# One fixed sequence for the MLP steps of all batches, with the attention of the next batch at set distances between them

## The chip, the cores and the metric

The kernel runs on one core of a Trainium2 chip. The metric is the device time of one execution in microseconds, taken from the first to the last instruction with what the launch adds around it. Before the change the median of three runs is 771.01 us (767.04 to 771.77). The profile is of one execution that took 770.31 us, with a span of 768.5 us from its first to its last instruction.

## The reference, cut to what matters

Four batches, 768 positions, 8 heads of 48, model width 384. Three layers follow one another, each batch by itself:

```python
f = sigmoid(f_logit)                                   # gated linear attention
for t in range(768):
    state = f[t, :, None] * state + outer(k[t], v[t])
    y[t] = q[t] @ state
x = y                                                  # (768, 384)
u = x + V.T @ (U.T @ x)                                # low-rank mix over positions
x = u + relu(u @ w_ch1) @ w_ch2                        # MLP, 384 -> 1536 -> 384
h = gelu(x @ w_in); a, g = halves(h)                   # second MLP with a spatial gate
out = x + (a * (w_sg @ layernorm(g) + b_sg)) @ w_out
```

The products of the two MLPs are made in three passes: each operand is held as a rounded high part and the rest (names ending in h and l), and high by high, high by low and low by high are added. So one logical matmul of the MLP is three in the trace. The weights arrive as 64-bit numbers and are narrowed on the chip: ScalarE scales the high word, VectorE shifts the low word and merges the two, then ScalarE rounds the high part and GpSimd subtracts for the rest.

## The kernel before, in words

The positions of a batch are cut into six chunks of 128 for the attention and into two halves of 384 for the MLP. The activations lie transposed in `xT[b]` (width on the partitions).

Attention of one chunk is five functions. `a_scan` (L308) takes the sigmoid on ScalarE, a backward and a forward scan of products on VectorE with three short VectorE instructions between them (`gmin` L328, `fall` L330, the reciprocal L331), and scales k and q by the results, mostly on GpSimd (L337, L338). `a_scores` (L343) multiplies k by q into two PSUM banks, masks them on VectorE (`am`, L353) and transposes k. `a_out` (L364) makes the outputs of the chunk from the state and from the masked scores, and the chunk's own k by v; ScalarE and GpSimd split the result into high and low part (`xh`, `xl`). `a_state` (L398) updates the state T on VectorE. `a_xt` (L412) turns the output into `xT`. `low_rank_sum` adds up the low-rank product after chunks 2 and 5 (every chunk for batch 0), and `low_rank_out` adds it to `xT`. `make_hl` then splits a half of `xT` into high and low part (`uh`, `ul`): three ScalarE and three GpSimd instructions.

The MLP of one half is 12 steps. Step f multiplies block f of the first weights with `uh` and `ul` into a bank `h` (9 matmuls, L79), applies ReLU on ScalarE (`ah`, L513), takes the rest on VectorE (`al`, L514), and then issues the second product (9 matmuls into three banks `ch`, L505) of the step before, from that step's `ah` and `al`. The second product of the last step of a half is issued after the loop, followed by three additions into `xT` (L530). After each step `fill(f)` issues other work. There are eight PSUM banks: two `h`, three `ch`, three `at`; the attention of batches 1 to 3 uses the three `at` banks.

What sets the order: every engine works its own queue in order. Inside a block of manual schedule the instructions of an engine keep the order in which the program issues them. Outside such a block a planner puts them in order from its own estimates when the program is built. It may also put instructions of later code between those of a block. Two blocks are manual before the change: batch 0's attention with the loading of weights (L538 to L585), and the MLP of batch 0's first half (L606 with `order`). Everything after is the planner's: the rest of the MLP with the attention of batches 1 to 3 (`attention_steps`, dealt out by counts in L598 to L602), the narrowing of the last weights during batch 3 (`fill` L626, `spatial` L632), and the second MLP (L713 on). `fill` of batch 0's first half also narrows the first weights ahead: `bank_middle`, `use_last` and `bank_first` for blocks f+3, f+2 and f+4.

Batch 0's sigmoid goes into a PSUM bank, that of batches 1 to 3 in place into the loaded tile, so the two can be told apart in the trace. A chunk of `fqk` and `v` is loaded two chunks ahead, into one of three buffers each.

Of the kernel before, what the change touches and what calls it, by code (L numbers as in the profile page):

```python
# [34 lines left out]
LIMIT = 1e-15  # L35
UNIT = 384
# [14 lines left out]
def kernel(  # L51
# [79 lines left out]
    def fast(st):  # L131
# [176 lines left out]
        def a_scan(b, c):  # L308
# [22 lines left out]
            ready = vec.reciprocal(fone[:, :, 0:1], gmin[:, i, :, None])  # L331
# [4 lines left out]
            with tc.issue_after(ready.ins) if b == 0 else nullcontext():  # L336
                pool.tensor_tensor(k, k, g.rearrange("p h t -> p (h t)"), op=ALU.mult)  # L337
# [126 lines left out]
        def attention_steps(b):  # L464
            def first():
                a_scan(b, 0)
            yield first
            for c in range(NCH):
                def s1(c=c):
                    a_scores(b, c)  # L470

                def s2(c=c):
                    if c + 1 < NCH:
                        a_scan(b, c + 1)
                    a_out(b, c)
                    nb, nc2 = divmod(b * NCH + c + 2, NCH)
                    if nb < B:
                        load(nb, nc2)

                def s3(c=c):  # L480
                    if c + 1 < NCH:
                        a_state(b, c)
                    a_xt(b, c)
                    low_rank_sum(b, c)
                yield s1
                yield s2
                yield s3

            def low(hf):
                low_rank_out(b, hf)  # L490
            yield lambda: low(0)
            yield lambda: low(1)

        def mlp(b, hf, fill, order=nullcontext):
            if (b, hf) not in hl:
                make_hl(work, b, hf)
            u = hl.pop((b, hf))
            ch = [bank("ch", [128, HT]) for _ in range(KD)]
            pend = None
# [7 lines left out]
            with order():  # L507
                for f in range(KF1):
                    hp = bank("h", [128, HT])
# [28 lines left out]
        with tc.manual_schedule():  # L538
# [14 lines left out]
            for c in range(NCH):  # L553
# [7 lines left out]
                if c:  # L561
                    a_xt(0, c - 1)
# [362 lines left out]
```

## Time and profile before

| | |
|---|---|
| median of 3 runs | 771.01 us |
| profiled execution, its span | 770.31 us, 768.5 us |
| TensorE matmul busy | 724.8 us (94%) |
| VectorE busy | 447.8 us (58%) |
| ScalarE, GpSimd busy | 258.3 us, 259.0 us (34% each) |
| mean granted TensorE clock | 0.969 |

Matmuls are pipelined, so busy time tells only that something was in the array; a step of 18 matmuls is judged by the time from its start to the next. Four stretches follow one another: batch 0's attention to 65.6 us, the MLP stream with the attention of the next batches and the last weights to 513.0 us, then the second MLP to the end. Within the MLP stream the starts of the halves can be found by the `h` matmuls: 65.6, 122.2, 205.9, 266.6, 321.1, 377.7, 433.9 and 475.4 us.

### The profile page before, as it was taken

The page shows a single profiled execution, that of the slowest core. Times are in us where ns is not written, and L with a number is a line of the kernel's source. Part 1 is how long each engine was busy: PE and PEld are TensorE (multiplying, and loading weights), DVE is VectorE, ACT ScalarE, POOL GpSimd, SP SyncE. Part 2 cuts the span into 40 slices and gives each one's busy share as a digit, 9 for nine tenths or more (in the row PEclk, how much of TensorE's full clock was granted, in tenths as well). Part 3 has the DMA queues.
Part 4 walks back from the last instruction along what each step waited for, and adds up shares of the span by engine and source line. Part 5 has one row for each costly group of instructions (what it writes and reads, how often), then busy time and mean ns, then how long its engine had stood idle before and what let it go on. Part 6 is the DMA issues. An engine that isn't in the chain of part 4 may idle for free.

```text
span 768.5 us, 11556 instructions
## 1 busy us (share of the span) xinstructions
PE 724.8 (94%) x4613; PEld 688.0 (90%) x4613; DVE 447.8 (58%) x789; ACT 258.3 (34%) x520; POOL 259.0 (34%) x273
## 2 busy tenths in 40 slices
PE   7977798998899999999999889999999999999996
PEld 5965688998899999999999789999989999999996
DVE  7857995655645555444533882138667447538632
ACT  2324551231322223222222551225444334524410
POOL 3312572323512122321201840326634435435130
PEclk8979899997999999999999999999999999999999
DMA  9991001131111131011100440210001001000101
GB/s 248 306 380 29 1 1 47 51 90 48 46 49 47 47 89 52 1 48 48 49 1 1 129 140 11 72 42 0 1 1 63 1 1 61 1 1 18 46 1 66
DMA packets 17934, 44.84 MB, mean 58 GB/s; under 512 B 2160, under 2 KB 9968, under 8 KB 17872
## 3 DMA queue, kind: packets, MB, share of 16 engines
q1 hardware_dynamic: 17872, 44.03, 18.9%
q8 instruction: 38, 0.62, 0.4%
q14 instruction: 24, 0.20, 0.1%
HBM read 39.30 MB, written 4.72 MB: 57 GB/s over the span
## 4 chain that ended last, share of the span: by engine, by line
PE 74%; DVE 15%; DMA 6%; ACT 2%; issue 1%; POOL 1%; SPq 1%; DVEq 0%; POOLq 0%; ACTq 0%
PE ps_h L79 22%; PE ps_ch L505 14%; PE ps_ch L79 12%; PE ps_at L79 12%; PE ps_at L373 4%; DMA fqk<-in_fqk_dram 3%; PE ps_at L349 2%; DVE fqk L332 2%; PE ps_at L370 2%; DVE z L248 1%; DVE g L325 1%; DMA xT<-in_fqk_dram 1%; DMA raw<-in_w_dram 1%; DVE al L514 1%; DVE z L101 1%; DVE raw L238 1%
## 5 line engine op out<-in xcount | busy, mean ns | idle before, releaser
L505 PE MATMUL ps_ch<-ah,w 128*128 128x384 f32 x576 | 163.2, 339 | 2.1 <-DVE xT L530 1.1
L79 PE MATMUL ps_h<-uh,w 128*128 128x384 f32 x576 | 126.0, 352 | 3.6 <-ACT w L277 2.6
L505 PE MATMUL ps_ch<-al,w 128*128 128x384 f32 x288 | 98.7, 343 | 15.9 <-DVE al L514 15.8
L514 DVE SCALAR_TENSOR_TENSOR al<-ps_h,ah 128x384 fp32r<-128x384 f32 x96 | 53.1, 554 | 98.6 <-ACT ah L513 97.5
L505 PEld LDWEIGHTS ps_ch<-ah,w 128*128 128x128 f32 x576 | 106.9, 190 | 3.0 <-ACT ah L513 3.0
L79 PEld LDWEIGHTS ps_h<-uh,w 128*128 128x128 f32 x576 | 102.1, 194 | 6.7 <-ACT w L277 3.3
L513 ACT ACTIVATE ah<-ps_h 128x384 fp32r<-128x384 f32 x96 | 46.9, 489 | 135.7 <-PE ps_h L79 130.5
L145 POOL TENSOR_TENSOR xl<-x,xh 128x384 fp32r<-128x384 f32 x18 | 21.0, 1165 | 156.6 <-ACT xh L144 156.6
L505 PEld LDWEIGHTS ps_ch<-al,w 128*128 128x128 f32 x288 | 54.9, 190 | 19.9 <-DVE al L514 19.8
L79 PE MATMUL ps_h<-ul,w 128*128 128x384 f32 x288 | 67.0, 340 | 0.0
L145 POOL TENSOR_TENSOR ul<-xT,uh 128x384 fp32r<-128x384 f32 x45 | 46.3, 1058 | 33.8 <-ACT uh L144 32.9
L145 POOL TENSOR_TENSOR gtl<-t,gth 128x384 fp32r<-128x384 f32 x32 | 32.7, 1024 | 73.6 <-ACT gth L144 73.6
L79 PEld LDWEIGHTS ps_h<-ul,w 128*128 128x128 f32 x288 | 53.0, 193 | 0.0
L337 POOL TENSOR_TENSOR fqk<-fqk,g 112x512 f32<-112x512 f32 x21 | 27.1, 1290 | 57.6 <-DVE gmin L328 26.8
L144 ACT ACTIVATE gth<-t 128x384 fp32r<-128x384 f32 x32 | 16.8, 525 | 78.0 <-DVE t L702 78.0
L353 DVE TENSOR_TENSOR am<-ps_at,mask 128x512 f32<-128x512 f32 x48 | 30.7, 682 | 16.4 <-PE ps_at L349 16.4
L145 POOL TENSOR_TENSOR vnl<-t,vnh 128x512 fp32r<-128x512 f32 x24 | 31.0, 1292 | 17.8 <-ACT vnh L144 17.8
L79 PE MATMUL ps_ch<-w,vnh 128*128 128x384 f32 x144 | 36.6, 335 | 0.1
L279 POOL TENSOR_TENSOR w<-z,w 128x384 fp32r<-128x384 f32 x24 | 24.8, 1054 | 35.0 <-ACT w L277 35.0
L79 PE MATMUL ps_at<-w,vnh 128*128 128x384 f32 x144 | 36.6, 334 | 0.0
L373 PE MATMUL ps_at<-v,am 128*128 128x48 f32 x288 | 35.9, 280 | 0.0
L373 PEld LDWEIGHTS ps_at<-v,am 128*128 128x128 f32 x288 | 35.4, 200 | 0.0
(218 smaller groups left out, 1555.4 us busy)
## 6 DMA issues: line engine op xcount, KB each, us to landing
fqk<-in_fqk_dram SPq DMA_DIRECT2D x19, 679.0 KB, 4.7
raw<-in_w_dram SPq DMA_DIRECT2D x24, 384.0 KB, 8.9
out_dram<-xT SPq DMA_DIRECT2D x24, 192.0 KB, 2.0
v<-in_v_dram SPq DMA_DIRECT2D x21, 192.0 KB, 3.3
raw<-in_w_in_dram SPq DMA_DIRECT2D x8, 384.0 KB, 3.5
z<-in_w_sg_dram SPq DMA_DIRECT2D x12, 192.0 KB, 2.4
xT<-in_fqk_dram SPq DMA_DIRECT2D x3, 679.0 KB, 11.6
raw<-in_w_out_dram SPq DMA_DIRECT2D x4, 384.0 KB, 3.2
```

Source lines behind the costliest of these rows:

```text
L79: pe.matmul(ps, lhsT=l, rhs=r, start=(i == 0), stop=(i == n - 1))
L144: act.activation(hi, src, ACTF.Copy)
L145: eng.tensor_tensor(lo, src, hi.bitcast(F32), op=ALU.subtract)
L279: pool.tensor_tensor(t[:, 1], s, t[:, 0].bitcast(F32), op=ALU.subtract)
L332: vec.tensor_tensor_scan(flat_f, f, fone.rearrange("p h t -> p (h t)"), 1.0, op0=ALU.mult, op1=ALU.max)
L337: pool.tensor_tensor(k, k, g.rearrange("p h t -> p (h t)"), op=ALU.mult)
L349: pe.matmul(sc[j][:, p, :], lhsT=e["k"][rows, p, :], rhs=e["q"][rows, p, :], start=True, stop=True)
L353: vec.tensor_tensor(am, sc[j], mask[:, None, :].to_broadcast([128, NP, C]), op=ALU.mult)
L373: pe.matmul(y[:, h * D:(h + 1) * D], lhsT=e["am"][h % 2][:, h // 2, :], rhs=vv[:, h * D:(h + 1) * D], start=(c == 0 and h == 0), stop=(h = ...
L505: pe.matmul(ch[d], lhsT=l, rhs=r, start=(f == 0 and i == 0), stop=(f == KF1 - 1 and i == 2))
L513: act.activation(ah, hp, ACTF.Relu)
L514: vec.scalar_tensor_tensor(al, hp, 0.0, ah.bitcast(F32), op0=ALU.max, op1=ALU.subtract)
```

## The change

One manual block is opened before the first load and closed only after the last step of batch 3 (`fixed.close()`); the last second product comes after it, then the second MLP as before. The MLP of all batches is 96 steps. The second product of a step is held in `pend` and issued in the next step across halves and batches too, and the additions into `xT` follow each bank's last matmul. For batches 0 to 2 a table says which step (0 to 23) issues which stage of the next batch's attention: chunk c is scanned at step `at[c]`, scored two steps later, put out three later with the load of chunk c+3 (before: c+2), `xT` and the low-rank sum four later; the state follows the output, or the scan of the next chunk if that is later. `at` is 9, 11, 12, 14, 16, 17 for batch 1 and 0, 3, 7, 10, 14, 17 for batches 2 and 3. Within a step the order is by rank: 0 narrowing of weights, 1 scan, 2 output, 3 scores and state, 4 the rest, 5 and 6 low-rank output and split. In batch 3 the raw data of a step are fetched two steps ahead. For batch 0 the scaling of k on GpSimd now waits for the reciprocal of the scan by a semaphore.

```diff
-            with tc.issue_after(ready.ins) if b == 0 else nullcontext():
-                pool.tensor_tensor(k, k, g.rearrange("p h t -> p (h t)"), op=ALU.mult)
+            decayed = pool.tensor_tensor(k, k, g.rearrange("p h t -> p (h t)"), op=ALU.mult)
+            if b == 0:
+                tc.add_manual_dep(decayed.ins, turned.ins.name,
+                                  mybir.DependencyInfo(mybir.DependencyClass.Sync, mybir.DependencyReason.DATA))
...
+        pend = [lambda: None]
+        def mlp(b, hf, fill):
             u = hl.pop((b, hf))
+            ch = []
             def second(f, a):
+                if f == 0:
+                    ch.extend(bank("ch", [128, HT]) for _ in range(KD))
                 for d in range(KD):
...
+                    if f == KF1 - 1:
+                        dst = xT[b][:, d, hf * HT:(hf + 1) * HT]
+                        vec.tensor_tensor(dst, ch[d], dst, op=ALU.add)
+            for f in range(KF1):
+                hp = bank("h", [128, HT])
...
+                act.activation(ah, hp, ACTF.Relu)
+                vec.scalar_tensor_tensor(al, hp, 0.0, ah.bitcast(F32), op0=ALU.max, op1=ALU.subtract)
+                pend.pop()()
+                pend.append(lambda f=f, a=(ah, al): second(f, a))
+                fill(hf * KF1 + f)
...
+        fixed = st.enter_context(ExitStack())
+        fixed.enter_context(tc.manual_schedule())
...
+            if b == 0:
+                for f in range(KF1):
+                    put(f, 0, narrow_ahead, f)
+                put(KF1 - 4, 4, load, 1, 2)
+            put(KF1 // 2, 5, make_hl, work, b, 1)
+            at = BEGIN[b > 0]
             for c in range(NCH):
+                put(at[c], 1, a_scan, b + 1, c)
+                put(at[c] + 2, 3, a_scores, b + 1, c)
+                put(at[c] + 3, 2, out_and_load, b + 1, c)
                 if c + 1 < NCH:
+                    put(max(at[c] + 3, at[c + 1]), 3, a_state, b + 1, c)
+                put(at[c] + 4, 4, rest, b + 1, c)
+            put(2 * KF1 - 2, 5, low_rank_out, b + 1, 0)
+            put(2 * KF1 - 2, 6, make_hl, work, b + 1, 0)
+            put(2 * KF1 - 1, 5, low_rank_out, b + 1, 1)
...
+        def fill_last(i):
+            if i < KF1:
+                hi, lo, _, at = todo[i]
+                c = slice(at, at + UNIT)
+                split(hi[:, c], lo[:, c], narrow_last(narrow_first(stage, here.pop(i), 128, UNIT))[0])
+            else:
+                split(*wsg[i - KF1], here.pop(i))
+            fetch_last(i + 2)
...
+            if i == KF1 // 2:
+                make_hl(work, B - 1, 1)
+            elif i == 2 * KF1 - 1:
+                make_hl(work2, 0, 0)
+                make_hl(work2, 0, 1)
...
+        for hf in range(2):
+            mlp(B - 1, hf, fill_last)
+        fixed.close()
+        pend.pop()()
```

## Rows read from the trace of the kernel before

**Rows 1.** The page's first part: busy time of each engine, share and instructions.

```profile
PE 724.8 (94%) x4613; PEld 688.0 (90%) x4613; DVE 447.8 (58%) x789; ACT 258.3 (34%) x520; POOL 259.0 (34%) x273
```

**Rows 2.** Windows: length, busy time (instructions) by engine, granted clock, DMA share, GB/s.

```profile
0.00:65.60 65.60, 55.15 (x411) 44.67 (x412) 44.43 (x85) 20.46 (x41) 16.82 (x25) 0.87 0.92 282
...
46.00:57.00 11.00, 10.60 (x55) 9.44 (x55) 4.84 (x11) 1.97 (x5) 1.95 (x2) 0.55 1.05 390
...
65.60:106.40 40.80, 31.79 (x164) 29.63 (x163) 39.57 (x76) 23.96 (x54) 23.17 (x23) 0.92 0.00 1
106.40:205.90 99.50, 90.45 (x641) 84.95 (x640) 60.55 (x100) 27.42 (x55) 33.90 (x29) 0.91 0.19 55
205.90:321.10 115.20, 111.79 (x801) 107.61 (x800) 63.39 (x104) 30.64 (x61) 32.00 (x28) 0.99 0.17 48
321.10:433.90 112.80, 109.78 (x801) 106.09 (x801) 53.79 (x91) 33.02 (x68) 27.53 (x26) 1.00 0.13 39
433.90:475.40 41.50, 39.18 (x218) 37.39 (x217) 27.37 (x50) 15.53 (x32) 14.01 (x12) 1.00 0.33 91
475.40:513.00 37.60, 37.60 (x218) 37.60 (x218) 8.45 (x16) 10.87 (x24) 12.26 (x12) 1.00 0.17 48
513.00:768.50 255.50, 249.11 (x1369) 240.08 (x1367) 150.24 (x274) 96.37 (x186) 99.26 (x122) 0.99 0.06 21
```

**Rows 3.** Timeline of TensorE: start, time, instruction, idle time before it and releaser.

```profile
46.40 1.99 PE L370 MATMUL ps_ch<-T,xT 112*128 112x96 f32 x8 [3.77 <-DVE T L410]
...
82.95 0.69 PE L505 MATMUL ps_ch<-al,w 128*128 128x384 f32 x1 [4.40 <-DVE al L514]
...
120.24 0.44 PE L505 MATMUL ps_ch<-al,w 128*128 128x384 f32 x1 [2.83 <-DVE al L514]
...
176.66 2.02 PE L370 MATMUL ps_at<-T,fqk 112*128 112x96 f32 x8 [2.89 <-DVE am L353]
...
309.04 0.76 PE L460 MATMUL ps_at<-vs,hs 128*128 128x384 f32 x3 [1.00 <-DVE hs L451]
...
432.38 0.44 PE L505 MATMUL ps_ch<-al,w 128*128 128x384 f32 x1 [2.66 <-DVE al L514]
```

**Rows 4.** Timeline of ScalarE in batch 0's attention.

```profile
40.37 0.63 ACT L318 ACTIVATE fqk<-fqk 112x512 f32<-112x512 f32 x1 [4.69 <-DMA fqk<-in_fqk_dram]
```

**Rows 5.** Timeline of VectorE in the same stretch.

```profile
41.09 1.22 DVE L325 TENSOR_TENSOR_SCAN g<-fqk,gone 112x511 f32<-112x511 f32 x1 [1.06 <-ACT fqk L318]
...
42.68 1.23 DVE L328 TENSOR_SCALAR gmin<-g 112x4 f32<-112x4 f32 x1
...
45.52 0.72 DVE L410 TENSOR_TENSOR T<-ps_ch,fall 48x192 f32<-48x192 f32 x2
```

**Rows 6.** Timeline of VectorE in batch 0's first half of the MLP.

```profile
79.06 3.37 DVE L238 TENSOR_SCALAR raw<-raw 128x384 int32<-128x384 int32 x2
```

**Rows 7.** Timeline of VectorE in batch 2, around one scan.

```profile
351.88 0.74 DVE L408 TENSOR_TENSOR T<-ps_at,T 48x192 f32<-48x192 f32 x2 [3.80 <-PE ps_at L392]
...
354.76 1.22 DVE L325 TENSOR_TENSOR_SCAN g<-fqk,gone 112x511 f32<-112x511 f32 x1
...
358.50 0.53 DVE L514 SCALAR_TENSOR_TENSOR al<-ps_h,ah 128x384 fp32r<-128x384 f32 x1
```

**Rows 8.** The page's groups: busy us, mean ns of one, idle before, releaser.

```profile
L514 DVE SCALAR_TENSOR_TENSOR al<-ps_h,ah 128x384 fp32r<-128x384 f32 x96 | 53.1, 554 | 98.6 <-ACT ah L513 97.5
...
L513 ACT ACTIVATE ah<-ps_h 128x384 fp32r<-128x384 f32 x96 | 46.9, 489 | 135.7 <-PE ps_h L79 130.5
...
L353 DVE TENSOR_TENSOR am<-ps_at,mask 128x512 f32<-128x512 f32 x48 | 30.7, 682 | 16.4 <-PE ps_at L349 16.4
```

**Rows 9.** Timeline of VectorE where batch 1's low-rank output ends.

```profile
204.10 4.02 DVE L328 TENSOR_SCALAR gmin<-g 112x4 f32<-112x4 f32 x1
```

**Rows 10.** Timeline of GpSimd there, and where batch 3's MLP begins.

```profile
202.21 5.88 POOL L145 TENSOR_TENSOR ul<-xT,uh 128x384 fp32r<-128x384 f32 x6
...
424.06 8.66 POOL L145 TENSOR_TENSOR ul<-xT,uh 128x384 fp32r<-128x384 f32 x8 [0.56 <-ACT uh L144]
```

More of the change, by code (lines that the diff above doesn't have):

```diff
@@ L1 @@
-from contextlib import ExitStack, nullcontext
+from contextlib import ExitStack
 import concourse.bass as bass
@@ new lines, in fast @@
+        load_first()
+        warm(4)
+        load(0, 2)
+        a_scan(0, 0)
+        get("u")
+        load(0, 3)
+        get("v0")
+        load(0, 4)
+        get("v1")
+        load(0, 5)
+        get(0, 1, 2)
+        a_scan(0, 1)
+        a_scores(0, 0)
+        warm(2)
+        for c in range(NCH):
+            if c + 2 < NCH:
+                a_scan(0, c + 2)
+            if c + 1 < NCH:
+                a_scores(0, c + 1)
+            if c in extra:
+                use_first(extra[c])
+                use_middle(extra[c])
+            if c:
+                a_xt(0, c - 1)
+            if c > 1:
+                low_rank_sum(0, c - 2)
+            if c == NCH - 1:
+                low_rank_sum(0, c - 1)
+            a_out(0, c)
+            warm(1, 1)
+            if c in extra:
+                use_last(extra[c])
+            if c + 1 < NCH:
+                a_state(0, c)
@@ new lines, in fast, with rest, out_and_load @@
+        low_rank_sum(0, NCH - 1)
+        a_xt(0, NCH - 1)
+        low_rank_out(0, 0)
+        make_hl(work, 0, 0, vec)
+        low_rank_out(0, 1)
+        use(1)
+        load(1, 0)
+        load(1, 1)
+        get(*range(3, KF1))
+        use_first(2)
+        use_middle(2)
+        bank_first(3)
+        warm(2)
+        def rest(b, c):
+            a_xt(b, c)
+            low_rank_sum(b, c)
+        def out_and_load(b, c):
+            a_out(b, c)
+            nb, nc3 = divmod(b * NCH + c + 3, NCH)
+            if nb < B:
+                load(nb, nc3)
@@ new lines, in narrow_ahead, with plan, put @@
+        def narrow_ahead(f):
+            if f + 3 < KF1:
+                bank_middle(f + 3)
+            if f + 2 < KF1:
+                use_last(f + 2)
+            if f + 4 < KF1:
+                bank_first(f + 4)
+        def plan(b):
+            steps = {}
+            def put(i, rank, fn, *args):
+                steps.setdefault(i, []).append((rank, fn, args))
+            if b == 0:
[4 more added lines that the diff above has]
+            at = BEGIN[b > 0]
@@ new lines, in plan, with fill @@
+                put(at[c] + 4, 4, rest, b + 1, c)
+            put(2 * KF1 - 2, 5, low_rank_out, b + 1, 0)
+            put(2 * KF1 - 2, 6, make_hl, work, b + 1, 0)
+            put(2 * KF1 - 1, 5, low_rank_out, b + 1, 1)
+            return steps
+        for b in range(B - 1):
+            steps = plan(b)
+            def fill(i):
+                for _, fn, args in sorted(steps.get(i, []), key=lambda x: x[0]):
+                    fn(*args)
+            for hf in range(2):
+                mlp(b, hf, fill)
@@ L640, in fast @@
-        low = wn.tile([PR, 1], F32, name="low")
-        vec.tensor_reduce(low, gmin.rearrange("p a b -> p (a b)"), axis=AX.X, op=ALU.min)
-        row = bank("at", [1, PR])
-        pe.transpose(row, low, ident[:PR, :PR])
-        good = wn.tile([1, 1], F32, name="good")
-        vec.tensor_reduce(good, row, axis=AX.X, op=ALU.min)
-        vec.tensor_scalar(flag, good, LIMIT, None, op0=ALU.is_gt)
-        mlp(B - 1, 0, fill)
-        mlp(B - 1, 1, spatial)
-        wsg = [[flat(x) for x in w1s[f]] for f in range(KF1)]
+        low = wn.tile([PR, 1], F32, name="low")
```

159 lines of the change are left out of this document (24 added, 135 removed).

## The prediction

> **What bounds the kernel now.** First the share of each engine: TensorE's matmuls are busy 94% of the span, no other engine above 58% [rows 1]. So the time goes only where TensorE idles or runs at its lower clock, and the windows by stage say where that is [rows 2]. The last half of the MLP is the measure of a stage without loss: 12 steps in 37.6 us, 3.13 us each, clock 1.00. Batch 2's MLP with batch 3's attention takes 112.8 us at clock 1.00; taking off 24 steps (75.2) and its long idle stretch of 2.66 us [rows 3], with some 0.4 us of short ones, leaves 34.6 us of attention, 5.8 us a chunk. By this measure batch 0's first ten steps (40.8 us against 29.7, the last second product not counted) lose 11 us, the rest of batch 0 (99.5 us) some 19 us, the next two batches 5 and 3 us, batch 3's first half 3.9, its second nothing, and the second MLP (255.5 us, clock 0.99 to its end) nothing that the change reaches.
>
> Then the timeline says what the losses are. In batch 0's attention TensorE waits 3.77 us for the state [rows 3], and ScalarE just before sat 4.69 us on a sigmoid whose data had not landed [rows 4]. That sigmoid works in place, so it belongs to batch 1: later work put between the steps of a block of fixed order. VectorE then does batch 1's scan, 1.06 us waiting for that sigmoid, 1.22 us of scan and a `gmin` of 1.23 us, ahead of the state [rows 5]. The same pattern returns in the first MLP steps: the shifts of two weights take 3.37 us [rows 6] and TensorE waits 4.40 us for `al`; and when three prefetched scans are finished in a row, 2.83 us, the longest of two such waits, at 120.24 [rows 3]. The lower clock follows: 0.55 on average from 46 to 57 us, 0.91 from 106.4 to 205.9 us [rows 2].
>
> **The change part by part.** The sum is made against the profiled 770.3 us (span 768.5), 0.7 us below the median of the runs.
>
> *Batch 0's attention, -7.3.* With one block nothing of batch 1 can stand there before its step 9. ScalarE loses the sigmoid, VectorE what it cost: 1.06 idle, then 1.14 from scan to the next start and 1.14 of `gmin`, 3.3 us [rows 5]. The state starts at 42.2 and not 45.52, and TensorE's wait of 3.77 shrinks to 0.5, or about 1 us with what ScalarE's lateness held up just before it. The following 11.0 us ran at 0.55, so they hold 6.05 us of full-speed work [rows 2]; I take 4.0 of the 4.95 us as gained, because VectorE's merging of weight 0 sits in the same stretch and stays. That needs the clock to hold over an idle stretch of about 1 us. The nearest rows are 1.00 us at 309 and 2.66 us at 432, each followed by a window at 1.00, and 3.77 at 46, followed by 0.55 [rows 2, 3]. Ends: -3.3 (the clock falls all the same) to -8.3. The new semaphore on the scaling of k delays GpSimd by the three short instructions of the scan, at no cost: the scores follow the scan by a chunk there; if that cover were gone, half a microsecond for each of six chunks.
>
> *First MLP steps, -4.5.* VectorE is busy 39.57 of 40.8 us [rows 2], so it is the bound and TensorE gains what VectorE sheds: a scan of 1.22, a `gmin`, and most of the 3.37 us of shifts (GpSimd runs batch 1's scaling of k and a weight's subtraction beside them), together some 4 us; and the 4.40 us wait was followed by a slow stretch that goes too. Against it: step 0's `al` now queues behind the narrowing of blocks 1 to 3, on VectorE and its ReLU on ScalarE likewise, which costs TensorE nothing as it waits for those weights anyway. Ends -2 and -6. Loads are further ahead (chunk 2 at step 8, behind all weights on SP's queue, with four steps until its scan).
>
> *Steps 9 to 23 of batch 0, -14.9.* The stages of batch 1 begin two steps earlier and are spread over 15 steps. TensorE's work from the end of step 9's first product is 15 x 3.13 - 1.6 + 34.6 = 80.0 us. What can hold it? `al` of step s+1 is needed when two more steps have passed: 6.2 us after step s's first product, plus the attention issued between. VectorE has it ready 1.2 us (ReLU and `al`, 0.49 and 0.55 with two handovers [rows 8]) plus its fill plus 0.6 us later. A scan is 3.74 us [rows 7]: 5.6 us, in time. Two places do stall. At step 12 the first output needs masks made behind chunk 1's scan: 0.6 us. At step 16 the transposes into `xT` come after scan 4 and the scores in the same step and need a bank of the three that is free only after the masks: VectorE is through 1.25 + 3.74 + 1.36 = 6.35 us after the first product, TensorE already at 3.0, a wait of 3.4 us; if it takes another bank that ScalarE frees earlier, 1.0. I take 2.0. The loads are no longer behind an output by one chunk, so the 2.89 us wait at 176.66 for masks of a late chunk goes [rows 3]. For the clock I keep one or two short falls, 2 us. Sum 84.6, ends 80 and 92.
>
> *Batches 1 and 2 of the stream, -0.6.* Each has 75.2 + 34.6 = 109.8 us of TensorE work. A scan alone is in time, but at steps 7 and 14 the state of the chunk before follows it on VectorE with no output between to give time: state up to 2.3 us (from the start of its additions to the next scan, less one `al` [rows 7]), so `al` comes at 7.7 against 6.4, 1.3 us each. At step 0 the three additions go before the scan: 0.7. `make_hl` at step 6 leaves three GpSimd subtractions beside step 7's `gmin`. The nearest row shows what that can do: a `gmin` of 4.02 us beside six subtractions of 5.88 us [rows 9, 10]. Here three end, by the same in-order count, about 0.6 us after `gmin` could start, which I take; ends 0 and 3. Sum 113.7 twice, 227.4 against 228.0.
> [...]
>
> *Batch 3, -2.9, and the end, +0.5.* Fetched two steps ahead, raw data are there; VectorE's narrowing and `al` fit into 3.13 us. The splits of batch 0 for the second MLP leave the place where eight subtractions in a row (8.66 us [rows 10]) ran beside the narrowing, and go to the very last step. There GpSimd queues one weight and three subtractions, 4 us, before the first block of the second MLP is complete; TensorE has 3.1 us of second products: +0.5, ends 0 and 2. 76.2 instead of 79.1 us, ends 75.5 and 80.
>
> Sum: -7.3 - 4.5 - 14.9 - 0.6 - 2.9 + 0.5 = -29.7, so **740.6 us**, range of this case alone 728 to 752.
>
> **The rivals.** *The clock falls as before.* [...] If dense attention, not idle time, brings it about, the forecast's gains of clock go: 4 in batch 0's attention, some 2 in the first steps, and 7 of the 9 (2 are kept in the sum): 753.6. For it: 0.91 over a stretch where idle time is only 9 of 99.5 us. Against: 1.00 in 321.1 to 433.9 with as much attention, if spread wider.
> [...]
>
> *VectorE's fixed queue holds TensorE at every scan (slower).* `al` behind a scan waits for its whole length. If the short instructions within each scan are blocked by GpSimd, as in [rows 9], the fill grows from 3.74 to 6 or 7 us and each of 18 scans costs as much as the wait at 120.24, 2.83 us [rows 3]: 51 us, of which 8 are counted, so 783. It decides from 2 us a scan, where the gains of 29.7 us are used up. For it: the planner of before could move `al` ahead of a scan and a fixed order can't. Against: at 354.76 a scan and `al` behind it took 3.74 us and no row of a long wait follows [rows 7].
>
> *Nothing changes.* The planner had already hidden what the plan hides, and what is gained early is given back by stalls between batches; or later work is still put between the fixed steps: 770.
>
> **How the numbers follow.** The forecast's mechanism 0.70 (740.6, 728 to 752), the clock 0.13 (754), nothing 0.09 (770), VectorE's queue 0.08 (783). The range leaves out the last two: 728 to 757. Faster by over 1% (7.7 us, about what a measurement tells from no change): 0.84; within 1%: 0.08, mostly of the third case; slower 0.08.
>
> **What would show it.** No in-place sigmoid before the MLP; the state of chunk 3 near 42 us and the first MLP matmul near 58 us, with clock 1.00 between; batch 1's first MLP matmul near 179 us (65.6 to 205.9 us before was 140.3, now about 121); batches 1 and 2 about 114 us each; TensorE's waits for `al` at steps 8 and 15 of them, of about 1 us, and one before a transpose at step 16 of batch 0. A stream with waits for `al` after each scan, or a clock under 0.95 over batch 0's second half, would prove it wrong.

## The result, and the profile after

The changed kernel takes 749.29 us in the median (747.63 to 750.88), beside 769.53 us of the kernel before on the same chip: a ratio of 0.9738, 95% interval 0.9693 to 0.9782. The forecast was 740.6 us, range 728 to 757. The profiled execution took 750.58 us with a span of 748.8 us, 19.7 us less than the 768.5 us before, where 29.7 us were forecast.

The page's first part of the changed kernel. TensorE's busy share went from 94% to 96% [rows 1]; it does the same 4613 matmuls.

```profile
PE 718.6 (96%) x4613; PEld 682.8 (91%) x4613; DVE 442.1 (59%) x789; ACT 257.5 (34%) x520; POOL 254.4 (34%) x273
```

Windows of the changed kernel by stage, the answer to [rows 2]: length, busy time (instructions) of TensorE, its weight loads, VectorE, ScalarE, GpSimd, granted clock, DMA share, GB/s. The stages are batch 0's attention, steps 0 to 8, steps 9 to 23, batches 1 and 2 in halves, batch 3 in halves, the second MLP.

```profile
0.00:60.40 60.40, 53.94 (x413) 42.50 (x413) 42.50 (x84) 20.12 (x40) 15.31 (x24) 0.92 1.00 301
...
60.40:96.50 36.10, 30.47 (x155) 29.15 (x154) 34.85 (x72) 22.30 (x51) 20.23 (x20) 0.86 0.04 10
96.50:184.40 87.90, 83.34 (x640) 79.61 (x639) 56.41 (x92) 26.70 (x54) 29.69 (x27) 0.98 0.21 62
184.40:241.30 56.90, 54.88 (x406) 52.69 (x405) 33.78 (x54) 15.42 (x31) 17.37 (x15) 1.00 0.16 48
241.30:297.50 56.20, 55.19 (x398) 53.45 (x397) 26.59 (x45) 14.99 (x30) 10.72 (x10) 1.00 0.17 48
297.50:357.50 60.00, 57.95 (x406) 55.60 (x405) 33.39 (x54) 15.42 (x31) 17.38 (x15) 0.94 0.16 46
...
413.70:453.40 39.70, 38.67 (x218) 37.34 (x218) 26.68 (x55) 15.81 (x35) 13.57 (x14) 1.00 0.43 125
453.40:493.10 39.70, 39.25 (x226) 38.89 (x226) 10.86 (x22) 14.62 (x33) 15.12 (x15) 1.00 0.19 55
493.10:748.80 255.70, 249.69 (x1370) 240.12 (x1368) 150.40 (x274) 97.11 (x188) 104.31 (x128) 1.00 0.06 21
```

Three more windows of the same kernel, around stretches in which the clock had fallen, to 0.50 and 0.51 of full speed.

```profile
65.00:75.20 10.20, 6.38 (x19) 5.84 (x20) 9.89 (x18) 5.92 (x14) 4.95 (x6) 0.50 0.00 1
143.50:147.00 3.50, 3.43 (x12) 3.43 (x13) 0.62 (x2) 0.98 (x2) 0.79 (x1) 0.51 0.00 0
341.40:348.40 7.00, 7.00 (x35) 6.47 (x34) 1.50 (x3) 1.28 (x3) 0.00 (x0) 0.51 0.00 0
```

The timeline of TensorE in the changed kernel at its longer waits, the answer to [rows 3]: start, time, instruction, idle time before it and releaser. The first is the state in batch 0's attention (3.77 us before); the second is for the `al` of step 0 (before, 4.40 for that of step 1); the third, at 106.78, is for the `al` of step 10, behind chunk 0's scan in step 9; the fourth stands at step 16, before a transpose. Batches 1 and 2 have two waits for `al` each; those of batch 1 came at 226.93 (1.73 us) and 262.22 (1.01 us).

```profile
42.36 1.10 PE L373 MATMUL ps_ch<-T,xT 112*128 112x96 f32 x8 [1.42 <-DVE T L413]
...
71.43 0.69 PE L479 MATMUL ps_ch<-al,w 128*128 128x384 f32 x1 [3.42 <-DVE al L490]
...
106.78 0.44 PE L479 MATMUL ps_ch<-al,w 128*128 128x384 f32 x1 [1.47 <-DVE al L490]
...
143.57 0.90 PE L419 MATMUL ps_at<-ident,x 128*128 128x128 f32 x3 [2.34 <-DVE am L356]
...
226.93 0.44 PE L479 MATMUL ps_ch<-al,w 128*128 128x384 f32 x1 [1.73 <-DVE al L490]
262.22 0.45 PE L479 MATMUL ps_ch<-al,w 128*128 128x384 f32 x1 [1.01 <-DVE al L490]
...
340.04 0.44 PE L479 MATMUL ps_ch<-al,w 128*128 128x384 f32 x1 [1.76 <-DVE al L490]
```

VectorE in the changed kernel, and one row of GpSimd: the state without a scan before it (at 45.52 us in [rows 5]); two shifts of a weight block with nothing beside them and two that run beside GpSimd's subtractions, with the `al` of step 0 behind, which answer to [rows 6]; and chunk 0's scan in step 9, with the `al` of steps 10 and 11 behind it.

```profile
41.49 0.72 DVE L413 TENSOR_TENSOR T<-ps_ch,fall 48x192 f32<-48x192 f32 x2
...
61.74 0.62 DVE L239 TENSOR_SCALAR raw<-raw 128x384 int32<-128x384 int32 x2
...
68.69 2.22 DVE L239 TENSOR_SCALAR raw<-raw 128x384 int32<-128x384 int32 x2
70.83 0.54 DVE L490 SCALAR_TENSOR_TENSOR al<-ps_h,ah 128x384 fp32r<-128x384 f32 x1
...
68.41 2.29 POOL L280 TENSOR_TENSOR w<-z,w 128x384 fp32r<-128x384 f32 x2 [1.98 <-ACT w L278]
...
102.13 1.61 DVE L326 TENSOR_TENSOR_SCAN g<-fqk,gone 112x511 f32<-112x511 f32 x1 [0.71 <-ACT fqk L319]
...
106.20 0.99 DVE L490 SCALAR_TENSOR_TENSOR al<-ps_h,ah 128x384 fp32r<-128x384 f32 x2
```

By stage, from the starts of the `h` matmuls (us). A second product of 1.56 us that stood at the end of each batch now stands behind the first product of the next one; batch 0's stretch is shorter and batch 3's longer by that much, which the "gain" column puts back.

| stage | before | after | gain | forecast |
|---|---|---|---|---|
| batch 0's attention | 65.6 | 60.4 | 5.2 | 7.3 |
| steps 0 to 8 | 39.2 | 36.1 | 3.1 | 4.5 |
| steps 9 to 23 | 101.1 | 87.9 | 11.6 | 14.9 |
| batch 1 | 115.2 | 113.1 | 2.1 | 1.5 |
| batch 2 | 112.8 | 116.2 | -3.4 | -0.9 |
| batch 3 | 79.1 | 79.4 | 1.3 | 2.9 |
| second MLP | 255.5 | 255.7 | -0.2 | -0.5 |

The large gains stand where they were forecast, each at 70 to 80% of its size, and batch 2 has become slower. The sign that was set for being wrong, a clock under 0.95 over batch 0's second half, did not come: it was 0.98 over steps 9 to 23.

### The profile page after: what moved, and what is told of

It is laid out like the page before. It is cut to its first block, busy times and chain, and to the rows that moved or that the text cites. A ratio compares the mean times of both kernels' runs of the same rounds, so it can differ in the third digit from the quotient of the medians.

```text
span 748.8 us, 11559 instructions
## 1 busy us (share of the span) xinstructions
PE 718.6 (96%) x4613; PEld 682.8 (91%) x4613; DVE 442.1 (59%) x789; ACT 257.5 (34%) x520; POOL 254.4 (34%) x273
## 4 chain that ended last, share of the span: by engine, by line
PE 73%; DVE 16%; DMA 5%; issue 2%; ACT 2%; SPq 1%; POOL 0%; DVEq 0%; ACTq 0%; POOLq 0%
PE ps_h L80 21%; PE ps_ch L479 13%; PE ps_ch L80 12%; PE ps_at L80 12%; PE ps_at L376 4%; PE ps_at L352 3%; DVE al L490 2%; DVE fqk L333 2%; DMA xT<-in_fqk_dram 2%; PE ps_at L373 2%; DVE z L249 2%; DVE g L326 1%; PE ps_at L395 1%; DMA v<-in_v_dram 1%; DVE raw L239 1%
## 5 line engine op out<-in xcount | busy, mean ns | idle before, releaser
L80 PE MATMUL ps_h<-uh,w 128*128 128x384 f32 x576 | 123.1, 349 | 2.2 <-ACT w L278 1.7
L479 PE MATMUL ps_ch<-al,w 128*128 128x384 f32 x288 | 98.3, 341 | 11.6 <-DVE al L490 11.6
L489 ACT ACTIVATE ah<-ps_h 128x384 fp32r<-128x384 f32 x96 | 47.0, 490 | 113.1 <-PE ps_h L80 111.8
L146 POOL TENSOR_TENSOR xl<-x,xh 128x384 fp32r<-128x384 f32 x18 | 18.4, 1023 | 101.8 <-ACT xh L145 101.8
L333 DVE TENSOR_TENSOR_SCAN fqk<-fqk,fone 112x512 f32<-112x512 f32 x18 | 35.0, 1945 | 1.7
L376 PE MATMUL ps_at<-v,am 128*128 128x48 f32 x288 | 34.3, 272 | 0.0
```

The source lines that it names most:

```text
L80: pe.matmul(ps, lhsT=l, rhs=r, start=(i == 0), stop=(i == n - 1))
L146: eng.tensor_tensor(lo, src, hi.bitcast(F32), op=ALU.subtract)
L333: vec.tensor_tensor_scan(flat_f, f, fone.rearrange("p h t -> p (h t)"), 1.0, op0=ALU.mult, op1=ALU.max)
L376: pe.matmul(y[:, h * D:(h + 1) * D], lhsT=e["am"][h % 2][:, h // 2, :], rhs=vv[:, h * D:(h + 1) * D], start=(c == 0 and h == 0), stop=(h = ...
L489: act.activation(ah, hp, ACTF.Relu)
```

## The experiments

All runs have the kernel before beside them on the same chip; its median was 768.8, 771.5 and 767.6 us in the three groups, so kernels of different groups are compared by ratio. Where a stage is judged, its time is from the profile of that run. Stage times (us):

| kernel | median | ratio and interval | att. 0 | 0-8 | 9-23 | b. 1 | b. 2 | b. 3 |
|---|---|---|---|---|---|---|---|---|
| one block | 751.42 | 0.9774 (0.9729-0.9818) | 60.6 | 36.1 | 89.9 | 110.8 | 109.7 | 86.8 |
| planner from batch 1 | 748.64 | 0.9739 (0.9711-0.9768) | 65.3 | 35.8 | 90.3 | 111.1 | 109.8 | 85.6 |
| scan put back | 754.51 | 0.9823 (0.9789-0.9857) | 67.6 | 35.9 | 86.4 | 113.1 | 113.1 | 79.6 |
| other steps | 745.79 | 0.9708 (0.9674-0.9743) | 58.1 | 37.2 | 87.6 | 112.8 | 112.5 | 79.5 |
| `al` first | 750.01 | 0.9705 (0.9664-0.9746) | 61.4 | 35.8 | 88.0 | 113.1 | 116.2 | 80.0 |
| transposes first | 743.40 | 0.9636 (0.9603-0.9669) | 60.3 | 36.2 | 83.8 | 113.1 | 113.1 | 79.4 |
| every three steps | 741.37 | 0.9606 (0.9573-0.9639) | 60.5 | 36.3 | 87.8 | 109.8 | 109.8 | 79.6 |
| three moves | 736.87 | 0.9550 (0.9515-0.9585) | 60.7 | 35.6 | 84.1 | 109.8 | 109.8 | 79.8 |
| added matmul | 748.89 | 0.9760 (0.9732-0.9789) | 58.4 | 36.0 | 87.9 | 113.1 | 116.2 | 79.5 |
| no semaphore | 745.62 | 0.9723 (0.9695-0.9752) | 58.2 | 37.1 | 87.6 | 113.1 | 113.1 | 79.4 |
| less merging | 742.34 | 0.9677 (0.9648-0.9705) | 58.0 | 31.6 | 87.6 | 113.1 | 116.2 | 79.4 |
| last version | 733.08 | 0.9548 (0.9520-0.9576) | 56.0 | 36.9 | 83.6 | 109.8 | 109.8 | 79.5 |

**One block.** The kernel before, with its two blocks of manual schedule made one that lasts through batches 0 to 2; its dealing out by counts stays, its second product too.

```diff
-        with tc.manual_schedule():
-            load_first()
...
+        fixed = st.enter_context(ExitStack())
+        fixed.enter_context(tc.manual_schedule())
+        load_first()
...
-                mlp(b, hf, fill, nullcontext if b or hf else tc.manual_schedule)
+                mlp(b, hf, fill)
+        fixed.close()
         at_cm.close()
```

> The kernel before with its two manual blocks made one that lasts to the end of batch 2's MLP; the stages of the attention are dealt out by before's counts, loads two chunks ahead, batch 3 as before. Theory A (the time went to scans of batch 1 put between the steps of batch 0, so one block is what counts): the first MLP matmul near 60 us as after the change (65.6 before), step 9 near 97, so 8 us gained there; 752 to 760 us in all. Theory B (the table of distances is what counts): without it nothing is gained, 765 to 775. [...]

The fixed order alone gives nearly the whole gain: batch 0's attention and steps 0 to 8 as in the changed kernel, steps 9 to 23 in 89.9 us (89.5 there, with the last second product counted as here). In batches 1 and 2 the old counts in fixed order are better than the new table; in the old order each scan from the second on is issued together with an output. Their windows:

```profile
186.60:297.40 110.80, 109.21 (x801) 106.19 (x800) 57.42 (x99) 30.20 (x61) 27.12 (x25) 1.00 0.17 49
297.40:407.10 109.70, 108.12 (x795) 104.72 (x794) 58.77 (x102) 32.93 (x68) 31.01 (x29) 1.00 0.13 36
```

Where the block ends and the planner takes over again, batch 3 takes 86.8 us against 77.8 in the changed kernel (79.4 less 1.56), with a wait of 3.36 us for `al` at 410.88. That is also more than the 79.1 us of the kernel before, where the planner had batch 3 as well; why it does worse behind a fixed batch 2 is not shown, so the 9 us are not the worth of the long block there.

**Planner from batch 1.** The changed kernel with the block closed after batch 0's 24 steps.

```diff
+            if b == 0:
+                fixed.close()
...
-        fixed.close()
         pend.pop()()
```

> The changed kernel with the block closed after batch 0, so the planner orders batches 1 to 3 again (with the table's distances only as the order of issue). Theory A: batch 0 as after the change (first MLP matmul of batch 1 near 184 us); batches 1 and 2 together 226 to 231 us as both kernels have it; 746 to 752 us. Theory B: batches 1 to 3 lose what the fixed order gave, 755 or more. If the planner puts scans of batch 2 into batch 0's fixed steps, the waits for al of before come back there, and batch 0 loses up to 5 us.

The total is that of the changed kernel. The planner does batches 1 and 2 in 111.1 and 109.8 us, better than the table in fixed order, and batch 3 in 85.6, worse by 6.2. The gain of the change comes from batch 0; from batch 1 on, against this kernel, it loses in batches 1 and 2 what it wins in batch 3. (Its profiled execution took 755.40 us at a mean clock of 0.976, the other four 745.83 to 749.41 at 0.985 to 0.991, so its 65.3 us of the first stage isn't compared.)

**Scan put back.** The changed kernel with batch 1's first load and scan issued in chunk 3's round of batch 0's attention, where the planner had put them before.

```diff
+            if c == 3:
+                load(1, 0)
+                a_scan(1, 0)
...
-                put(at[c], 1, a_scan, b + 1, c)
+                if b or c:
+                    put(at[c], 1, a_scan, b + 1, c)
```

> The changed kernel with one thing put back: batch 1's first load and first scan stand in batch 0's attention, before the narrowing in chunk 3's round, where the planner had them. Theory A: ScalarE's sigmoid waits there for its data some 4 to 5 us, the first MLP matmul comes at 64 to 66 us instead of 60.4, and the kernel at 752 to 756 us. Theory B: the scan is hidden there, 749. Theory C: only if the clock falls longer than the 6.8 us of the changed kernel.

Here ScalarE waits 4.73 us for the data of that sigmoid (4.69 in [rows 4]), the outputs of chunk 4 wait 5.75 us for the state, and the first MLP product comes at 67.6 us, 7.2 later than in the changed kernel. The timelines of ScalarE and TensorE in this kernel:

```profile
39.30 0.63 ACT L319 ACTIVATE fqk<-fqk 112x512 f32<-112x512 f32 x1 [4.73 <-DMA fqk<-in_fqk_dram]
...
48.14 1.14 PE L373 MATMUL ps_ch<-T,xT 112*128 112x96 f32 x4 [5.75 <-DVE T L413]
```

That is the wait of 3.77 us in [rows 3], brought back by that one stage: the cause of the first term is shown. It is longer than before, and the product later than the 64 to 66 us expected, since here both of the stage's scans run ahead of the weight's merging. The same run shows what the stage costs at its new place: without chunk 0's scan in step 9 the wait of 1.47 us at step 11 is gone, and steps 9 to 23 take 86.4 us and not 87.9.

**Other steps.** The changed kernel with chunks 2 and 4 of batches 2 and 3 one step earlier, so that those scans share a step with an output.

```diff
-BEGIN = [(9, 11, 12, 14, 16, 17), (0, 3, 7, 10, 14, 17)]
+BEGIN = [(9, 11, 12, 14, 16, 17), (0, 3, 6, 10, 13, 17)]
```

> The changed kernel with two numbers of the table for batches 2 and 3 changed: chunk 2 begins at step 6 (was 7) and chunk 4 at step 13 (was 14), so that the state of the chunk before falls into the step of that chunk's output. Theory A (al waits at steps 8 and 15 because state and scan stand together on VectorE with no output on TensorE to cover them): the four waits of 1.73, 1.01, 1.76 and 1.01 us go, and the fall of the clock behind the third with 3.4 us: 741 to 744 us. Rival (a scan alone makes al late, wherever it stands): four waits as long as before at the new places, 749. Theory C: gain only where the clock fell, batch 2 alone.

The four waits did not go; they are now 1.42 and 0.98 us at step 6's state and 1.02 and 1.01 at step 17's. Timelines of this kernel, VectorE, GpSimd and TensorE:

```profile
216.42 4.91 DVE L413 TENSOR_TENSOR T<-T,fall 48x192 f32<-48x192 f32 x2
221.36 1.02 DVE L490 SCALAR_TENSOR_TENSOR al<-ps_h,ah 128x384 fp32r<-128x384 f32 x2
...
215.84 1.29 POOL L341 TENSOR_TENSOR fqk<-fqk 112x512 f32<-112x512 f32 x1 [1.52 <-DVE fqk L333]
217.09 1.02 POOL L146 TENSOR_TENSOR xl<-x,xh 128x384 fp32r<-128x384 f32 x1
218.06 3.06 POOL L146 TENSOR_TENSOR ul<-xT,uh 128x384 fp32r<-128x384 f32 x3
...
221.98 0.45 PE L479 MATMUL ps_ch<-al,w 128*128 128x384 f32 x1 [1.42 <-DVE al L490]
```

In step 6 the state's two multiplications (L413) take 4.91 us, 1.28 in the changed kernel at 225.00, while GpSimd works without a break from 215.84 to 221.1: this step also has the subtractions of `make_hl`. In step 17 a scan and a state stand without an output again. They do so in step 10 too, and there no wait follows; TensorE has three transposes and the six products of the low-rank sum in that step, 1.37 us. So a wait arises in two ways, and the kernel with every three steps, below, takes both away.

**`al` first.** The changed kernel with the narrowing of blocks 2 and 3 moved behind step 0's `al`.

```diff
-        use_first(2)
-        use_middle(2)
-        bank_first(3)
...
+            if f == 0:
+                use_first(2)
+                use_middle(2)
+                bank_first(3)
```

> The changed kernel with one move: VectorE's narrowing of gate blocks 2 and 3, which the changed kernel issues before step 0 of the stream, is issued in step 0 after that step's al subtraction. [...] Rival B (the al is late because VectorE is blocked by GpSimd wherever it stands, or the narrowing is due there in any order): the wait only moves to steps 1 to 3, where the blocks' narrowed parts are then late, and the time stays within 2 us of 749.3.

The wait of 3.42 us goes, and one of 2.07 us comes a step later, for the ReLU, which on ScalarE stands behind the spreading of block 4, and that waits for VectorE's merging (`z`, L249). Steps 0 to 8 take 35.8 us, 0.3 less. Rival B is right for this move: it changes where TensorE waits, not how long the steps take. The timelines of TensorE and ScalarE:

```profile
74.25 0.44 PE L479 MATMUL ps_ch<-ah,w 128*128 128x384 f32 x1 [2.07 <-ACT ah L489]
...
73.27 0.52 ACT L243 ACTIVATE ps_at<-raw 128x384 f32<-128x384 f32 x1 [2.31 <-DVE z L249]
73.72 0.47 ACT L489 ACTIVATE ah<-ps_h 128x384 fp32r<-128x384 f32 x1
```

**Transposes first.** In step 16 of batch 0 the transposes of batch 1's chunk 2 go ahead of the scores.

```diff
-                put(at[c] + 4, 4, rest, b + 1, c)
+                put(at[c] + 4, 2.5 if b == 0 and c == 2 else 4, rest, b + 1, c)
```

> The changed kernel with one move: in step 16 of batch 0's steps the transposes and low-rank sum of batch 1's chunk 2 are issued ahead of the scores of another chunk, not after them. Theory A (the wait of 2.34 us at 143.57 is the transposes' for VectorE's am, which that step's scores feed, and the fall of the clock from 143.5 to 146.9 follows from it): the wait falls under 0.8 us, the clock holds there, and the time is 745 to 748 us. Rival B (TensorE waits at this step whichever comes first, because the output of chunk 3's predecessor is late on VectorE): a wait of over 1.5 us stays in the step, and the time is within 1.5 us of 749.3.

No wait over 0.7 us is left in step 16, the clock holds (1.00 over the window below), and steps 9 to 23 take 4.1 us less: the wait and half of the 3.5 us at 0.51 that followed it. The window of steps 9 to 23 in this kernel:

```profile
96.50:180.30 83.80, 81.59 (x640) 78.05 (x639) 56.24 (x92) 26.55 (x54) 29.92 (x27) 1.00 0.23 65
```

The time fell below what was expected because batch 2 took 113.1 us and not 116.2. Its `al` wait of 1.76 us is still there at 335.88, but the clock did not fall behind it in that run. The timeline of TensorE at that wait, and the window around it:

```profile
335.88 0.44 PE L479 MATMUL ps_ch<-al,w 128*128 128x384 f32 x1 [1.76 <-DVE al L490]
...
335.00:343.00 8.00, 7.12 (x54) 6.75 (x55) 4.22 (x7) 1.56 (x3) 0.00 (x0) 1.00 0.00 1
```

**Every three steps.** The table for batches 2 and 3 with one distance, so that the scans from the second on share a step with an output and a state, and `make_hl` one step later.

```diff
-BEGIN = [(9, 11, 12, 14, 16, 17), (0, 3, 7, 10, 14, 17)]
+BEGIN = [(9, 11, 12, 14, 16, 17), (0, 3, 6, 9, 12, 15)]
...
-            put(KF1 // 2, 5, make_hl, work, b, 1)
+            put(KF1 // 2 + (b > 0), 5, make_hl, work, b, 1)
```

> The changed kernel with the steps of the attention stages in batches 1 and 2 set every three steps (0, 3, 6, 9, 12, 15 in place of 0, 3, 7, 10, 14, 17), so that each scan but the first shares its step with an output and with the state of the chunk before, and with the narrowing of the second half's input one step later, out of the state's step. Theory A (a step's al is late where VectorE has a scan and a state and TensorE no output to cover them, or where a short VectorE instruction is blocked by GpSimd's subtractions): the four al waits of 1.0 to 1.8 us at steps 8 and 15 go, batches 1 and 2 take 110 to 111 us each in place of 113.1 and 116.2, and the time is 741 to 744 us. Rival B (VectorE's work for a step is late at whichever step the scan stands, since a step is shorter than scan plus al): waits of the same number and size come at other steps and the two batches keep 113 us each; time 746 to 749 us.

Theory A: no wait over 0.5 us is left in either batch, and both run at what the forecast gave as their TensorE work, 109.8 us. The windows of the two batches:

```profile
184.60:294.40 109.80, 109.51 (x802) 106.22 (x802) 61.04 (x99) 30.24 (x61) 27.43 (x25) 1.00 0.18 50
294.40:404.10 109.70, 109.41 (x801) 106.12 (x800) 60.67 (x99) 30.23 (x61) 27.43 (x25) 1.00 0.09 26
```

**Three moves.** The last three edits together.

```diff
+            if f == 0:
+                use_first(2)
...
+BEGIN = [(9, 11, 12, 14, 16, 17), (0, 3, 6, 9, 12, 15)]
...
+                put(at[c] + 4, 2.5 if b == 0 and c == 2 else 4, rest, b + 1, c)
```

> The three moves at once (the narrowing of gate blocks 2 and 3 behind step 0's al, the transposes of batch 1's chunk 2 ahead of the scores in step 16, and the steps every three in batches 1 and 2). If each wait is a loss by itself, the gains add: 3 to 6, 1 to 4 and 5 to 8 us below 749.3, so 733 to 740 us. If they share a cause that moves along (VectorE late in whichever place), the sum is less than half of that: 743 to 748 us.

The gains add. Against the changed kernel the spans fell by 9.1 us (every three steps) and 7.5 (transposes first), of which 3.1, batch 2's clock, is the same time twice; with all moves the span is 734.5, 14.3 us less.

**Added matmul.** One more matmul of the identity ahead of chunk 4's outputs in batch 0.

```diff
+            if c == 4:
+                warm(1)
             a_out(0, c)
```

> The changed kernel with one added matmul of the identity by 384 columns (its result is not used) on TensorE just before the outputs of batch 0's chunk 4, where TensorE idled 1.42 us at 42.36 for the state. Theory A (that idle time is what lets the granted clock fall from 44.5 to 51.4): idle time there under 0.5 us, no fall between 42 and 60, the first MLP product at 57 to 58.5 instead of 60.4, time 746 to 748 us. Rival B (the fall comes without regard to this wait; another run of the same code held the clock over 1.40 us): the clock falls for 3 to 7 us all the same, first MLP product at 60 to 61, time 748 to 751 us.

The wait there is 0.67 us, not under 0.5, and the clock held; the first MLP product comes at 58.4. Windows of 42 to 58 us in this kernel, then in the changed kernel and in the one with other steps, whose code up to there is the changed kernel's:

```profile
42.00:58.00 16.00, 13.85 (x95) 10.62 (x94) 8.83 (x20) 6.54 (x16) 1.96 (x2) 1.00 1.03 397
```

```profile
42.00:58.00 16.00, 14.36 (x87) 11.76 (x87) 5.82 (x13) 3.31 (x8) 1.95 (x2) 0.79 1.04 398
```

```profile
42.00:58.00 16.00, 13.24 (x93) 10.62 (x94) 8.96 (x20) 6.46 (x15) 1.96 (x2) 1.00 1.03 385
```

The third had a wait of 1.40 us there and held the clock. Of nine profiles with that wait (1.42 us in the changed kernel, 1.40, 1.41 and 1.40 with other steps, no semaphore and less merging) the clock fell in six, with the first MLP product at 60.3 to 61.4 us, and held in three, with it at 58.0 to 58.2; in the two with 0.67 us and none it held (1.00 over 42 to 58 us). This fits theory A but doesn't show it, and the time of the whole kernel, 748.89 us, is not told apart from the changed kernel's.

**No semaphore.** Batch 0's scaling of k without its wait for the reciprocal.

```diff
-            if b == 0:
+            if b == B:
                 tc.add_manual_dep(decayed.ins, turned.ins.name,
```

> The changed kernel without the semaphore by which batch 0's scaling of k on GpSimd waits for the reciprocal of the scan. The forecast put that wait at nothing. Theory A: without it GpSimd starts some 1 us earlier in six chunks and TensorE gains nothing; first MLP product within 0.7 us of 60.4, time 748 to 751 us. Rival B (the semaphore keeps GpSimd from blocking VectorE's three short instructions): without it gmin, fall or the reciprocal take 1 to 2.5 us in the chunks, the first MLP product comes at 61.5 to 66, time 751 to 756 us. Rival C (the wait cost the path half a microsecond a chunk): first MLP product at 57 to 59, time 745 to 748 us.

Its first MLP product at 58.2 us looks like rival C, but the clock held in this run (1.00 over 42 to 58 us); the kernel with other steps, which has the semaphore and whose clock held too, has it at 58.1. The semaphore costs nothing, as forecast. Nor does its absence: no short instruction of a scan grew in batch 0's attention (`gmin` at most 0.17 us in both, `fall` 0.15, the reciprocal 0.18).

**Less merging.** The first of two merging instructions is left out for weight blocks 2 to 5, so that this kernel computes with incomplete weights there.

```diff
-                vec.scalar_tensor_tensor(zi, zi, 3, low, op0=ALU.logical_shift_left, op1=ALU.bitwise_or)
+                if i not in (2, 3, 4, 5):
+                    vec.scalar_tensor_tensor(zi, zi, 3, low, op0=ALU.logical_shift_left, op1=ALU.bitwise_or)
```

> The changed kernel without the first of the two merging instructions on VectorE (0.56 us, two of them a block) for gate-free MLP weight blocks 2 to 5; the low words of these four weights are left out of the sums. Nothing else moves. Theory A (VectorE's narrowing is the bound of steps 0 to 8, so that any order of it leaves the time as it is): eight instructions of 0.56 us, 4.5 us, come off VectorE before step 4, the wait of 3.42 us at 71.43 falls by 1 to 2.2 us, and the time from the first MLP product to that of step 9 falls from 36.1 to 31 to 33.5 us; time 744.5 to 747 us. Rival B (the wait is one of order, and TensorE is the bound besides): the wait shortens by at most the 1.1 us ahead of it and the stretch keeps 35 us or more; time 748 to 750 us.

Theory A: eight instructions of 0.56 us less on VectorE, 4.5 us, and steps 0 to 8 are 4.5 us shorter (31.6), at clock 1.00. The whole kernel is faster than the 744.5 to 747 us expected, as in its profile the clock also held ahead of the first product (58.0 us; 1.00 over 42 to 58). The window of these steps and the timeline of TensorE at the wait that was 3.42 us:

```profile
58.00:89.60 31.60, 27.90 (x155) 26.55 (x154) 30.67 (x65) 22.45 (x52) 20.46 (x20) 1.00 0.21 62
```

```profile
66.28 0.45 PE L480 MATMUL ps_ch<-al,w 128*128 128x384 f32 x1 [0.89 <-DVE al L491]
```

VectorE is busy 97% of the stretch here as in the changed kernel (34.85 of 36.10 us), so the time follows VectorE's work, though the clock held in the one and not in the other.

**Last version.** Every three steps and transposes first, and in batch 0 the state ahead of the last part of a weight's narrowing.

```diff
-            if c in extra:
-                use_last(extra[c])
             if c + 1 < NCH:
                 a_state(0, c)
+            if c in extra:
+                use_last(extra[c])
```

> The steps every three in batches 1 and 2 and the transposes of batch 1's chunk 2 ahead of the scores in step 16, as in the run of the three moves at once (736.9 us), without the move of the narrowing of blocks 2 and 3 behind step 0's al, and with batch 0's state issued ahead of the last part of a weight's narrowing (VectorE then doesn't sit 0.59 us for ScalarE's part of w_v before the state). Theory A (the waits add, the move of the narrowing was worth nothing): TensorE's wait of 1.42 us before chunk 4's outputs falls under 0.5 us, the first MLP product comes at 57 to 59.5, and the time is 733 to 736.5 us. Rival B (the move of the narrowing did hold the gain there, or the part put behind the state is late in its turn for the low-rank sum): 737 to 741 us.

VectorE no longer idles 0.59 us ahead of the state for ScalarE's part of that weight. TensorE doesn't wait before chunk 4's outputs, and the first MLP product comes at 56.0 us, a microsecond earlier than expected. Windows of the first three stages:

```profile
0.00:56.00 56.00, 50.29 (x411) 40.12 (x412) 41.84 (x83) 20.27 (x40) 15.82 (x24) 0.97 1.00 293
56.00:92.90 36.90, 30.41 (x155) 29.04 (x154) 35.23 (x72) 22.58 (x52) 20.47 (x20) 0.91 0.20 57
92.90:176.50 83.60, 81.47 (x640) 78.09 (x639) 56.04 (x92) 26.43 (x54) 29.73 (x27) 1.00 0.24 65
```

Its ratio is the best of all but not told apart from that of the three moves (0.9548 and 0.9550). Both beat the changed kernel.

## Why the prediction was right, and where its sizes were off

**The mechanism** is shown for batch 0's attention: one scan put back there costs 7.2 us to the first MLP product. For the rest of batch 0 it is shown that the fixed order brings the gain, as one block alone has a ratio of 0.9774 beside the changed kernel's 0.9738; which piece of later work cost how much there was not tested piece by piece. From batch 1 on the change adds nothing against the kernel before (2.1 - 3.4 + 1.3 us in batches 1 to 3), and against old counts in fixed order its table loses in batches 1 and 2. The time lies between the forecast and the 753.6 us of the clock rival, and not by errors that cancel, since all three large gains fell short.

**Batch 0's attention** (7.3 forecast, 5.2 measured). The state came at 41.49 us (42.2 forecast) and TensorE's wait was 1.42 us (0.5 to 1). The step that failed is "that needs the clock to hold over an idle stretch of about 1 us": the clock fell, to 0.79 in the mean over 42 to 58 us. In the profiles where it held the first product came at 58.0 to 58.2 (58.4 with the added matmul), a gain of 7.2 to 7.6: the size was right for a held clock. In two of them steps 0 to 8 took 37.1 and 37.2 us and gave 1 us of that back. The forecast had weighed two rows in which the clock held and one of a long wait; the kernel before also had a nearer one against it, waits of 1.11 and 0.89 us with the clock at 0.59 behind them. What decides between the two is not settled. TensorE in the kernel before at these waits, and the window behind them:

```profile
210.26 0.41 PE L505 MATMUL ps_ch<-ah,w 128*128 128x384 f32 x1 [1.11 <-DVE xT L530]
211.56 0.44 PE L505 MATMUL ps_ch<-al,w 128*128 128x384 f32 x1 [0.89 <-DVE al L514]
...
213.00:217.00 4.00, 4.00 (x16) 4.00 (x15) 0.18 (x1) 0.49 (x1) 0.00 (x0) 0.59 0.00 0
```

**Steps 0 to 8** (4.5 and 3.1). That VectorE is the bound was right and is shown: its busy time over these steps fell by 3.1 us (37.97 to 34.85), as the time did; with less merging it fell again by 4.2, and the time by 4.5. The window of these steps in the kernel before:

```profile
65.60:104.80 39.20, 30.18 (x155) 28.18 (x154) 37.97 (x74) 22.91 (x52) 21.57 (x21) 0.91 0.00 1
```

The failed size is "most of the 3.37 us of shifts": all shifts of the stretch together fell by 2.0 us (12.29 to 10.30), for twice two shifts of a block still take over 2.2 us beside GpSimd's subtractions, not the 0.62 of an undisturbed pair. Nor did the slow stretch go that was to go with the 4.40 us wait: around the wait of 3.42 us there are 10.2 us at clock 0.50, and they begin ahead of it, at 65.0. "Costs TensorE nothing" of step 0's `al` behind the narrowing so looked wrong; the run with `al` first shows that it was right in sum, since the time is VectorE's in either order.

**Steps 9 to 23** (14.9 and 11.6, 3.3 short). The wait before the transposes at step 16 was there, 2.34 us (2.0 forecast), and a fall of the clock worth 1.7 (2). The 0.6 us of step 12's first output for its masks did not come. The step that failed is "5.6 us, in time" for `al` behind a scan: the first one, behind the scan in step 9, came 1.47 us late at step 11. VectorE began that scan only at 102.13, behind the narrowing of step 8 and 0.71 us of idle time for ScalarE's sigmoid, and took 4.1 us for it, not 3.74. The rest lies in the term of 80.0 us for TensorE's work: in the run with the transposes first it is 81.59 less 1.60 for step 9's first product plus 1.56 for the last second product, 81.55, with 0.8 us of short waits besides. Together (1.47 - 0.6) + 0.3 - 0.3 + 1.55 + 0.8 = 3.2 of the 3.3.

**Batches 1 and 2** (113.7 each; 113.1 and 116.2). The two waits a batch stand right behind the steps that were named, 1.73 and 1.01 us where 1.3 was forecast. The forecast's own terms add up to 1.2 + 3.74 + 2.3 + 0.6 = 7.8 and not 7.7, which changes little. In step 7 `gmin` took 0.80 us and not 0.17, the 0.6 us forecast beside `make_hl`. The 3.1 us more of batch 2 are the clock behind the wait of 1.76 us: 0.51 over 7 us. Over the same wait, in other runs, it held (batch 2 in 113.1); in the runs without the waits it held each time (batch 2 in 109.8, at 1.00 with every three steps and in the last version). That the waits themselves were needless, the forecast did not see: a table with a distance of three steps has none.

**Batch 3** (2.9 and 1.3). Idle time of 39.70 - 38.67 and 39.70 - 39.25, 1.5 us in waits of at most 0.63, where the forecast had `al` fitting into each step. **The end** (-0.5 and -0.2) was small as forecast.

**The rivals.** The clock rival held in part: the mean granted clock rose only from 0.969 to 0.979. The 9 us in its sum are the 99.5 us at 0.91 of [rows 2], the 2 in the first steps an estimate within the 3.3 us that 40.8 at 0.92 give; for the changed kernel, length times one less the clock gives an estimate of 4.8, 5.1 and 1.8 us for batch 0's three stretches (60.4 us at 0.92, 36.1 at 0.86, 87.9 at 0.98). VectorE's fixed queue costs batches 1 and 2 two waits each of 1.0 to 1.8 us, and batch 0 one of 1.47, not 2.83 a scan.

## What to carry to other kernels

Where a fixed order gains, look first for the work that a planner had put between its steps, and test the block apart from the table: here the block brought the time, and the table lost time until its distances let each scan from the second on share a step with an output. In a stretch that another engine bounds, as VectorE does steps 0 to 8, the reordering moved TensorE's wait and left the time (36.1 and 35.8 us); work taken off that engine shortened it (31.6). Price a stall once with the clock held and once with it fallen, as both came with the same wait (1.40 to 1.42 us in batch 0, 1.76 in batch 2).

## What was not expected of the hardware

One short VectorE instruction took as long as several of GpSimd's beside it. Of the state's two multiplications in the kernel with other steps (4.91 us) the first took 3.83 us, while GpSimd ran one instruction after the other; the same instruction took 0.90 us in the changed kernel at 225.00. VectorE in the kernel with other steps, then in the changed kernel (both multiplications):

```profile
216.42 3.83 DVE L413 TENSOR_TENSOR T<-T,fall 48x192 f32<-48x192 f32 x1
```

```profile
225.00 1.28 DVE L413 TENSOR_TENSOR T<-T,fall 48x192 f32<-48x192 f32 x2
```

The 3.83 us are longer than any one of GpSimd's instructions beside it (1.02 to 1.29 us).

The granted clock fell or held over one and the same wait, in batch 0 (1.40 to 1.42 us: six profiles with a fall, three without) and in batch 2 (1.76 us in the changed kernel and with the transposes first: four profiles with a fall and the batch in 116.2 us, three without and 113.1). This moves a run by about 2 to 3 us at each place.
